# Crossbar transposes for a third of a batch, and VectorE steps merged over heads, tiles and spectra, in a fused attention and gated convolution

## The chip, the cores and the metric

The kernel runs on one core of a Trainium2 chip (trn2). The metric is device time in microseconds (us) of one execution, the median of several runs. The core has TensorE (matmuls and transposes, into PSUM banks), VectorE, ScalarE, GpSimd and SyncE, each with an instruction stream of its own that is worked off in order; they meet through semaphores. DMA engines move data between HBM and the on-chip memory (SBUF) and inside SBUF. Loads are issued here by GpSimd, stores and transposing copies by SyncE.

## What is computed

The reference is attention with a local window and a few global keys, followed by a long convolution with gates on both sides. There are 4 batches, 8 heads, 768 positions and 64 elements to a head, so a model width of 512.

```
scores = q @ k^T / sqrt(64) - slope[h] * dist       # kept: 0 <= i-j < 96, or j < 8
x      = concat over heads of softmax(scores) @ v    # (4, 768, 512)
x1, x2, x3 = split(x @ w_proj)                       # each (4, 768, 512)
c      = irfft(rfft(x2, axis=seq) * rfft(filter, axis=seq))
out    = (x1 * c * x3) @ w_out
```

## The kernel before

**Attention.** For each of four batches the 768 positions are worked in seven key tiles of 112 rows, in three groups `c`: tiles (0, 1), (2, 3), (4, 5, 6). q and k arrive as rows (`qn`, `kn`, one buffer each for all batches) and are needed with the head's elements on the partitions (`QT`, `KT`). `turned` (L672 and on) transposes them on TensorE (L679) into a PSUM bank and has VectorE or ScalarE copy them out (L309). `crossed` (L662 and on) has SyncE issue a DMA transpose instead (L669). `XB` (L207) names the (batch, group) pairs that go this way: the second and third group of the last batch. `scores` forms a key tile against its window of queries for two heads at a time, 64 rows each (L720), ScalarE takes the exponential (L748) into `E`, and VectorE multiplies by a mask that holds window, slopes and global keys (L760). In batch 0 the mask is added on TensorE instead (L707). `values` multiplies by v (L778, L783); VectorE takes the reciprocal of the sums (L808) and normalises (L802). Each v tile has the rows of the global keys below its own 112; a copy inside SBUF, issued by SyncE, puts them there once v's tile 0 has landed (`load_global`, L325 through `load`).

**Gates and convolution.** The normalised x is turned (L825, or by DMA, L835) into `xT`. `gate` multiplies xT by a 128-column tile of the first and third part of w_proj for one half of the positions (L870), has x1 and x3 copied out (L313, L879), and multiplies both on VectorE (L881). The convolution splits the sequence by symmetries (`butterfly`, L846 to L857), projects (L944), takes a small Fourier transform as matmuls (L634), copies six spectra out (`X`), multiplies by the filter's spectrum as complex numbers (`spectra`, L1081 to L1098), transforms back (L965, L968), mixes halves (L1036 to L1042), joins and multiplies by the gates (L1056 to L1061), and multiplies by w_out (L996). The filter's spectrum and the tables of sines are made in the kernel during batch 0.

**The order.** Nothing is scheduled at run time. The functions record operations with their reads and writes; `ORDER` (L40 to L88) is a list of them, one word each, such as `86P45`: operation 86, on TensorE, into PSUM banks 4 and 5. The word's letter also chooses VectorE or ScalarE where a copy can go to either. Each engine works its words in the order of the list, and GpSimd and SyncE issue their DMAs in that order. `i13b0` stands for thirteen dummy matmuls while the first loads are under way; a dummy exponential (`6A`, L371) brings ScalarE's table of exponentials back after the sines.

Of the kernel before, what the change touches and what calls it, by code (L numbers as in the profile page):

```python
# [16 lines left out]
P = 128  # L17
# [23 lines left out]
4V 0S 1A 2S 3A 21G 12V 13V 28V 10G 30A 29A 31A 15V 33V 11A i13b0 76P0 32A 34G 17G 19V 41G 18G 9V 40G 39G 42G 20V 66A  # L41
63A 24V 61A 72P1 46G 14V 35G 25V 70P2 26V 23A 22V 7G 64A 47G 73A 48G 45G 67A 60A 38G 77V 86P45 80V 74P3 52G 44G 90P01
43G 16V 75V 71A 78P2 79V 50G 49G 110P6 111V 51G 91P 81A 65A 62A 112P3 113A 88P 87P 89A 55G 261G 108P2 8V 219P6 220A
92P 93A 114P3 156P7 94P45 96P 109V 95P 27V 115V 122P23 262G 97A 69V 260G 221V 157V 214P0 82P45 259G 222V 123A 158P7
159V 84P 116P23 215A 216V 160P1 117A 83P 161V 120P67 53G 217V 154P1 5V 155V 118P23 258G 270G 85A 269G 121A 119A 268G
36S 267G 162P01 273G 98P67 275G 68V 99V 100V 37S 164P45 163A 165A 103P23 104V 105V 276G 166P67 167A 168P01 274G 124P23
125V 126V 129P45 130V 131V 56G 57G 169A 106P6 107A 101P7 102A 127P2 128V 175P01 176V 132P3 58G 133V 170P45 59G 139P3
145P2 263G 223A 54G 177V 178P0 171V 362P1 493G 492G 172V 173P4 224A 179V 227V 229P5 207V 226A 266G 277G 141A 174V
360P0 491G 272G 218A 134P3 208V 201V 271G 363A 230A 361A 364A 150P4 185P0 228V 186P1 358P7 489G 490G 147A 6A 278G 210V
200V 203V 188A 209V 231V 359V 202V 211V 225V 152A 181P2 136A 232A 140P1 369P67 142V 375P45 204V 183A 279G 143V 370A  # L50
390P3 135P2 388P1 499G 498G 212V 365A 501G 376A 500G 187V 137A 391V 389V 372P67 180P0 366P23 373A 392P45 191P1 138V
182A 374V 264S 434P0 436P6 367A 371V 393A 193A 395P23 189V 396A 510G 438P7 435V 205V 398P45 399A 196P0 437V 439V
449P67 450A 401P23 402A 198A 184V 507G 504G 206V 285P1 281P4 394V 213V 506G 286A 505G 283P5 446P23 440P01 397V 443P67
282A 447A 296P4 307P2 284A 298P3 297A 289P4 441A 299A 149P5 144P0 302P3 592P1 290A 400V 494G 151A 195P5 300P4 451V
509G 444A 265S 377V 368V 722G 146A 403V 234V 235V 236V 237V 383P67 448V 308A 190P0 502G 303A 238V 153V 301A 239V 148V
192A 384V 240V 197A 378P23 721G 385V 287P4 241P0 593A 590P5 242A 379V 409P67 723G 591A 194V 246P1 247A 380V 288A 442V
404P23 243P0 244A 248P5 726G 588P1 724S 410V 411V 199V 412P4 405V 249A 594V 719G 445V 406V 457P67 381P5 245V 595A 250V
407P0 589A 408A 382A 452P23 386P1 387A 458V 233V 459V 618P0 460P5 619A 453V 738G 413V 454V 251P67 252A 461V 496S 620P1
621V 508G 255P23 305V 253A 420P0 257A 455P1 292V 456V 256A 631P67 632A 605P45 294P3 422A 295A 414P1 416A 495S 664P0
254V 665A 304V 666P2 482V 668P3 667A 602P67 603A 735G 483V 669V 424P1 484V 306V 309P0 310A 478P2 425P3 528P0 280G 485V  # L60
291V 606A 679P45 486V 480A 426A 311V 427A 529A 676P67 419P2 677A 415P3 293V 417A 421A 511P0 607V 512A 312V 680A 487V
524P1 525A 313P0 462P2 418V 670P67 678V 428V 604V 681V 728G 599P45 464A 321P3 733G 323P1 314A 322A 600A 671A 515P2
315P3 516A 325P0 324V 317P1 318A 327P4 488V 326V 429P5 328A 497G 430P0 319P2 320A 431A 432A 601V 736G 513P1 514A 316V
628P23 633V 596P45 673P67 672V 597A 629A 730G 526P0 674A 329V 463P1 468P4 465A 330V 473P5 475A 625P23 626A 622P67 846S
734G 890S 821P1 848S 729G 527A 423V 331V 433V 732G 334V 727G 332V 472P5 623A 539P2 630V 477P3 519P0 845S 335V 333V
822V 847S 540A 467P1 520A 720G 474A 819P2 737G 338V 336V 470V 339V 469A 517P0 337V 479A 627V 537P5 518A 613P67 614V
820A 538A 349P1 350A 718G 598V 615V 889S 624V 675V 817P0 532P2 818A 340P5 503G 685P67 686V 824V 341A 533A 687A 608P01
609V 530P5 531A 823V 892S 610V 471V 891S 682P23 683V 476V 639P01 640V 684V 346P4 347A 634P67 616P5 617A 641V 828P23
829A 855P01 856A 635V 611P4 535V 343P5 893P23 688S 894A 636V 612V 481V 902P67 344A 852P01 355P4 903A 830V 853A 534V
637P2 541V 638V 642P3 643V 352P5 542V 649P3 689S 904V 356A 353A 834P67 835A 521V 825P01 826A 522V 854V 654P2 656A  # L70
655P5 739G 645P4 647A 644P6 690S 523V 657A 651A 466V 536V 659P2 661A 712V 711V 646A 648V 702P7 704A 714V 858P45 859A
896P23 713V 831P01 832A 697P6 857V 715V 345S 897A 543P7 707P4 709A 836V 557P5 555P0 556A 744P1 551P2 545P4 553P3 699A
716V 860V 348S 549P0 650P6 558A 550V 833V 554A 717V 827V 658V 725S 544A 552A 731G 547P5 342S 548A 546A 560V 559V 753P0
691P7 895V 849P45 652A 754A 850A 899P23 693A 900A 755P6 756A 660P0 745A 561V 837P45 838V 839A 740P7 851V 840P23 757P6
564V 701P1 841V 842V 662A 901V 843S 351S 703A 861P23 908P45 898V 905P01 741A 565V 862V 692P7 758A 909V 910A 863V 696P6
357S 906V 562V 864P23 907V 706P0 759P1 694A 563V 761P7 865V 866A 568V 742P4 743A 762A 766P5 768P2 569V 767A 844S 566V
911S 585P3 663V 354S 746P4 567V 760A 764V 867S 579P7 912S 748P1 769A 582P2 573P5 708A 763V 580A 868S 770V 749A 570P7
747A 583A 576P2 765V 705V 771V 750V 774P4 786P1 586A 782P3 571A 751V 913S 775A 778P7 870P0 710V 752V 577A 783A 787A
935V 934V 936V 772P2 780P4 773A 781A 937V 930P3 932A 776P2 777A 938V 872A 784P1 785A 885P4 880P3 958P0 779A 789V 945P7
939A 788V 940V 941P1 959A 946A 790V 791A 943P0 944A 653V 875P7 695V 942A 954P2 578S 955A 949P0 950A 793V 877A 956P1  # L80
957A 947P2 948A 572S 794V 792V 967P7 968A 587S 869P0 581S 969P1 970A 882A 795V 797V 924P2 796V 951V 971V 960P7 961A
952V 962P1 963A 925P3 871A 927A 879P7 881A 915P0 972V 953V 884P3 584S 965V 988P7 887A 964V 698A 574A 886A 966V 888V
973P6 974A 700V 992P4 993A 989A 873V 798V 805P1 994P6 995A 990P3 975P4 991A 997V 996V 977P5 978A 979P7 980A 874P6
802P3 808P7 883V 876A 799P6 998V 814P5 878V 976A 981V 982V 575S 999A 926A 914P2 806A 1001V 811P1 983V 984A 1002V 1000V
929P4 917A 815A 800A 801S 919P6 807S 986V 803A 809A 920P7 985V 987V 1005V 816S 810S 1003V 804S 1006V 812A 931A 1004V
1013P3 1018V 916A 813S 921A 933V 918V 922A 1007P2 1008A 1016V 1009S 923V 1014A 1015S 928V 1017V 1010P7 1019V 1020P2
1011V 1012S 1021V 1022S 1023P3 1024A 1026P7 1027A 1025S 1028S 1029P2 1030A 1031S
# [112 lines left out]
class Fused:  # L200
# [6 lines left out]
    XB = ((3, 1), (3, 2))  # L207
# [31 lines left out]
    def buffers(self):  # L239
# [30 lines left out]
        pp = t("pp", [P, 2, 4, DM])  # L270
        self.p1, self.p2 = ([pp[:, x, 2 * i:2 * i + 2] for i in range(2)] for x in range(2))
# [418 lines left out]
    def scores(self, hp, gi, near=False):  # L690
# [60 lines left out]
        if near:  # L751
            return
        mk = self.mask[:, 2 * hp:2 * hp + 2]
        if gi < 2:
            mk = mk[:, :, self.STEP * gi:self.STEP * (gi + 2)].rearrange("p h (t c) -> p h t c", t=2)[:, :, :, 0:n]
            w = 2 * W
        else:
            eo, mk = et[:, :, at:at + W + 16], mk[:, :, self.STEP:self.STEP + W + 16]
            w = 2 * (W + 16)
        g.op("V", dve(w, 2), lambda _: nc.vector.tensor_mul(eo, eo, mk),  # L760
             r=[("mask", 2 * hp), ("mask", 2 * hp + 1)], w=[("E", hp, gi)], name="masked")
# [98 lines left out]
    def gate(self, b, j, s):  # L860
        nc, g, h = self.nc, self.g, self.S // 2
        gt = self.gt[b % 2]
        xs = [("xT", i, c) for i in range(2) for c in ((0, 1) if s == 0 else (1, 2))]
        pts = []
        for o in (0, 2 * self.DM):
            bk = g.bank()

            def run(_, o=o, bk=bk):
                for c in range(4):
                    nc.tensor.matmul(bk.f32()[:, 0:h], self.w[:, c, o + P * j:o + P * j + P],  # L870
                                     self.xT[:, c, h * s:h * s + h], start=(c == 0), stop=(c == 3))
            g.op("P", pe(*[h] * 4), run, acq=[bk], r=xs + [("w", o // P + j)], name="gate")
            pts.append(bk)
        x1, key = self.x1[self.turn4 % 4], ("x1", self.turn4 % 4)
        self.turn4 += 1
        g.op("AV", self.evac(h), lambda e: self.times(e, x1, pts[0].f32()[:, 0:h], X1_SCALE),
             use=[pts[0]], w=[key], name="x1")
# [7 lines left out]
    def attention(self, b):  # L885
        self.b = b
        self.g.batch = (self.PERIOD * (b - 1 + self.SHIFT), self.PERIOD * self.LONG)
        for c in range(3):
# [18 lines left out]
            for i in range(4):  # L907
                self.scores(i, c, b == 0 and c < self.NEAR)
# [327 lines left out]
```

## Time and profile before

| | |
|---|---|
| median of 3 runs | 165.59 us (164.84 to 165.88) |
| the profiled execution | 165.6 us |
| its span, first to last instruction | 163.9 us |
| TensorE busy | 156.0 us, 95% |
| VectorE busy | 149.6 us, 91% |
| ScalarE busy | 149.7 us, 91% |
| GpSimd busy | 73.9 us, all before 82 us |
| granted TensorE clock | 1.00 throughout |

The profile names engines PE (TensorE matmuls), PEld (TensorE weight loads), DVE (VectorE), ACT (ScalarE), POOL (GpSimd) and SP (SyncE); a q behind the name (SPq) is the engine's queue that issues a DMA or waits. A line such as `PE bank L870` is work on the tile `bank`, recorded at line 870. The chain of waits follows back from the last instruction what each had to wait for; pieces in it have a start and a length in us. The list of waits tells which engine and line waited for which, the total in us, how often, and the longest. In a timeline each row has a start, a length, the engine, the line, the tile written and the tiles read, shapes, and how many instructions are merged. Busy time of TensorE is from modelled ends, so a busy TensorE may still be short of its full rate.

### The profile page before, as it was taken

The page shows a single profiled execution, that of the slowest core. Times are in us where ns is not written, and L with a number is a line of the kernel's source. Part 1 is how long each engine was busy: PE and PEld are TensorE (multiplying, and loading weights), DVE is VectorE, ACT ScalarE, POOL GpSimd, SP SyncE. Part 2 cuts the span into 40 slices and gives each one's busy share as a digit, 9 for nine tenths or more (in the row PEclk, how much of TensorE's full clock was granted, in tenths as well). Part 3 has the DMA queues.
Part 4 walks back from the last instruction along what each step waited for, and adds up shares of the span by engine and source line. Part 5 has one row for each costly group of instructions (what it writes and reads, how often), then busy time and mean ns, then how long its engine had stood idle before and what let it go on. Part 6 is the DMA issues. An engine that isn't in the chain of part 4 may idle for free.

```text
span 163.9 us, 4281 instructions
## 1 busy us (share of the span) xinstructions
PE 156.0 (95%) x1619; PEld 95.3 (58%) x1619; DVE 149.6 (91%) x339; ACT 149.7 (91%) x325; POOL 73.9 (45%) x101
## 2 busy tenths in 40 slices
PE   6798999999999999899999999999999999999990
PEld 2455678665456875455566755665754654574550
DVE  3788869999999999999999999999999999999970
ACT  4688899999999999999999999999999798999931
POOL 7999999985599999978700000000000000000000
PEclk9999999999999999999999999999999999999999
DMA  4999999999999999999995545000444270010586
GB/s 109 196 147 125 166 172 166 158 173 206 178 173 158 153 150 146 140 172 155 156 139 102 76 93 184 14 0 4 130 128 107 78 270 0 4 64 0 206 326 238
DMA packets 91684, 21.97 MB, mean 134 GB/s; under 512 B 84288, under 2 KB 88720, under 8 KB 91664
## 3 DMA queue, kind: packets, MB, share of 16 engines
q0 software_dynamic: 74960, 11.82, 98.7%
q1 hardware_dynamic: 14624, 9.37, 21.0%
q10 hardware_dynamic: 2080, 0.52, 1.8%
q8 instruction: 12, 0.20, 0.4%
q14 instruction: 8, 0.07, 0.1%
HBM read 24.64 MB, written 6.29 MB: 189 GB/s over the span
## 4 chain that ended last, share of the span: by engine, by line
PE 55%; DVE 25%; POOL 6%; ACT 5%; DMA 4%; issue 2%; POOLq 0%; ACTq 0%; DVEq 0%
PE bank L870 16%; PE bank L996 12%; PE bank L944 8%; DVE E L760 5%; PE bank L634 4%; DMA qn<-in_q_dram 4%; DVE xn L802 3%; PE bank L720 3%; PE bank L778 3%; PE bank L965 3%; POOL kn L325 3%; PE bank L783 2%; PE bank L707 2%; ACT E L748 1%; DVE xT L309 1%
## 5 line engine op out<-in xcount | busy, mean ns | idle before, releaser
L870 PE MATMUL bank<-xT,w 128*128 128x384 f16 x256 | 48.5, 326 | 0.6 <-DVE KT L309 0.6
L748 ACT ACTIVATE E<-bank 128x832 f16<-128x832 f32 (+2 forms) x64 | 44.6, 785 | 1.2 <-PE bank L720 1.2
L870 PEld LDWEIGHTS <-w 128*128 128x128 f16 x256 | 23.6, 98 | 17.1 <-issue 1.9
L325 POOL DMA_DIRECT2D vn<-in_v_dram x28 | 23.4, 852 | 4.0 <-DMA wo<-in_moe_w_out_dram 1.7
L325 POOL DMA_DIRECT2D kn<-in_k_dram x27 | 22.7, 866 | 0.7 <-issue 0.3
L996 PE MATMUL bank<-wo,y 128*128 128x512 f16 (+1 forms) x100 | 22.9, 370 | 0.0
L760 DVE TENSOR_TENSOR E<-E,mask 128x832 f16<-128x832 f16 (+1 forms) x36 | 21.4, 617 | 0.4 <-ACT E L748 0.4
L325 POOL DMA_DIRECT2D qn<-in_q_dram x21 | 19.0, 920 | 1.4 <-PE bank L944 1.4
L879 ACT CAST g<-bank 128x384 f16<-128x384 f32 x30 | 15.8, 542 | 0.3 <-PE bank L870 0.3
L313 ACT ACTIVATE x<-bank 128x384 f16<-128x384 f32 x31 | 16.1, 548 | 0.0
L313 ACT ACTIVATE ot<-bank 128x512 f32<-128x512 f32 (+1 forms) x23 | 12.9, 608 | 3.1 <-PE bank L996 1.9
L802 DVE TENSOR_TENSOR xn<-bank,rc 128x512 f16<-128x512 f32 (+1 forms) x20 | 15.2, 763 | 0.2
L778 PE MATMUL bank<-vn,E 128*128 128x65 f16 x224 | 15.3, 193 | 0.0
L313 ACT ACTIVATE ab<-bank 128x512 f16<-128x512 f32 x24 | 15.1, 688 | 0.1
L996 PEld LDWEIGHTS <-y 128*128 128x128 f16 x100 | 9.4, 98 | 9.9 <-issue 0.3
L778 PEld LDWEIGHTS <-E 128*128 128x128 f16 x224 | 14.0, 97 | 1.9
L783 PE MATMUL bank<-vn,E 128*128 128x65 f16 x192 | 15.0, 193 | 0.0
L720 PE MATMUL bank<-QT,KT 64*128 64x208 f16 (+1 forms) x224 | 14.9, 245 | 0.0
L309 ACT CAST X<-bank 128x512 f16<-128x512 f32 x24 | 14.0, 659 | 0.1
L783 PEld LDWEIGHTS <-E 128*128 128x128 f16 x192 | 13.2, 97 | 0.8 <-issue 0.2
L309 ACT CAST eo<-bank 128x384 f16<-128x384 f32 x28 | 12.4, 566 | 0.8 <-PE bank L968 0.8
L720 PEld LDWEIGHTS <-KT 64*128 64x128 f16 x224 | 8.4, 94 | 6.4 <-issue 3.9
(158 smaller groups left out, 337.4 us busy)
## 6 DMA issues: line engine op xcount, KB each, us to landing
out_dram<-ot SPq DMA_DIRECT2D x23, 256.0 KB, 2.5
qn<-in_q_dram POOLq DMA_DIRECT2D x21, 128.0 KB, 5.7
vn<-in_v_dram POOLq DMA_DIRECT2D x24, 112.0 KB, 5.7
kn<-in_k_dram POOLq DMA_DIRECT2D x23, 112.0 KB, 5.6
w<-in_moe_w_proj_dram POOLq DMA_DIRECT2D x4, 256.0 KB, 6.4
ot<-in_q_dram ACTq DMA_DIRECT2D x2, 256.0 KB
w<-in_moe_w_proj_dram POOLq DMA_DIRECT2D x1, 512.0 KB, 7.8
wo<-in_moe_w_out_dram POOLq DMA_DIRECT2D x1, 512.0 KB, 8.1
```

What stands on the lines that cost most here:

```text
L309: {"A": nc.scalar.copy, "V": nc.vector.tensor_copy, "G": nc.gpsimd.tensor_copy}[e](out, in_)
L313: self.nc.scalar.mul(out, in_, c)
L325: return self.g.op(eng, 0.57 + 0.00035 * nbytes[0] if eng == "G" else 0.5, lambda _: e.dma_start(dst, src), w=w, r=r, nbytes=nbytes, name= ...
L720: nc.tensor.matmul(bs[hh].f32()[:, off:off + w], self.KT[hs, hp, P * m:P * m + P], self.QT[hs, hp, KL * m:KL * m + w], start=(off == 0 and ...
L748: nc.scalar.activation(dst, src(), Act.Exp, scale=self.scale)
L760: g.op("V", dve(w, 2), lambda _: nc.vector.tensor_mul(eo, eo, mk), r=[("mask", 2 * hp), ("mask", 2 * hp + 1)], w=[("E", hp, gi)], name="ma ...
L778: nc.tensor.matmul(o[:, n, hh], ef[:, at:at + P], vt[:, t, 2 * hp + hh, 0:D + 1], start=first, stop=(t == 0), skip_group_check=True)
L783: nc.tensor.matmul(o[:, n, hh], ef[:, at:at + P], vt[:, t - 1, 2 * hp + hh, 0:D + 1], start=False, stop=True, skip_group_check=True)
L802: nc.vector.tensor_mul(to, o[:, :, :, 0:D].rearrange("p i (t h) d -> p i t h d", h=2), rc.rearrange("p i (t h) o -> p i t h o", h=2).to_br ...
L870: nc.tensor.matmul(bk.f32()[:, 0:h], self.w[:, c, o + P * j:o + P * j + P], self.xT[:, c, h * s:h * s + h], start=(c == 0), stop=(c == 3))
L879: first = g.op("AV", {"A": act(h), "V": 0.0005}, lambda e: nc.scalar.copy(x3, pts[1].f32()[:, 0:h]) if e == "A" else None, use=[pts[1]], w ...
L996: nc.tensor.matmul(bk.f32()[:, 0:cw], y[:, c, P * t:P * t + P], self.wo[:, c, cs], start=(c == 0), stop=(c == 3))
```

## The change

Five things change.

1. `XB` takes in the first group of the last batch, so its three q tiles and two k tiles are transposed by DMA.
2. The mask of one group is multiplied into `E` for four heads in one VectorE instruction, instead of two heads. It moves from `scores` to a function of its own, `masked`.
3. `gate` handles two column tiles at once: four matmul blocks, four copies to SBUF, and one VectorE product of twice the length. A product straight from PSUM, possible before, is not left.
4. The complex products of a batch run over the four spectra 0 to 3 in one instruction each, instead of over pairs: two products and one sum of 2048 elements. They follow all four spectra. The spectra 4 and 5 keep their two products.
5. `ORDER` is another one from beginning to end, with other choices of engine and bank.

```diff
-    XB = ((3, 1), (3, 2))
+    XB = ((3, 0), (3, 1), (3, 2))
...
+    def masked(self, j, gi):
+        t0, n, W = self.GRP[gi][0], self.N, self.GW[gi]
+        et, mk = (x[:, 4 * j:4 * j + 4] for x in (self.EE.rearrange("p i h c -> p (i h) c"), self.mask))
...
+        self.g.op("V", dve(w, 2), lambda _: self.nc.vector.tensor_mul(et, et, mk),
+                  r=[("mask", 4 * j + i) for i in range(4)], w=[("E", 2 * j + i, gi) for i in range(2)], name="masked")
...
-    def gate(self, b, j, s):
+    def gate(self, b, jp, s):
...
+        for j in range(2 * jp, 2 * jp + 2):
...
+            g.op("AV", self.evac(h), lambda e, x3=x3, bk=pts[1]: self.copy(e, x3, bk.f32()[:, 0:h]),
+                 use=[pts[1]], w=[("g", b % 2, j, s)], name="x3")
+        x3 = gt[:, js, h * s:h * s + h]
+        g.op("V", dve(2 * h, 2), lambda _: nc.vector.tensor_mul(x3, x3, self.x1p[:, k:k + 2]),
+             r=[("x1", k + i) for i in range(2)], w=[("g", b % 2, j, s) for j in range(2 * jp, 2 * jp + 2)], name="g")
...
         self.spectra(b, (2, 3))
+        self.products(False)
         self.spectra(b, (4, 5))
+        self.products(True)
...
+    def products(self, real):
+        nc, g, X, DM = self.nc, self.g, self.X, self.DM
+        ss = (4, 5) if real else (0, 1, 2, 3)
+        ks, xs = [("X", s) for s in ss], X[:, ss[0]:ss[-1] + 1]
...
+        g.op("V", dve(2048, 2), lambda _: nc.vector.tensor_mul(
+            p1, xs, self.h1[:, 0:4:2][:, :, None].to_broadcast([P, 2, 2, DM])), r=rs, w=[("p1", 0), ("p1", 1)], name="prod")
+        g.op("V", dve(2048, 2), lambda _: nc.vector.tensor_mul(p2, xs, hs), r=rs, w=[("p2", 0), ("p2", 1)], name="prod")
+        g.op("V", dve(2048, 2), lambda _: nc.vector.tensor_add(xs, p1, p2[:, :, ::-1]),
+             r=[(k, i) for k in ("p1", "p2") for i in range(2)], w=ks, name="sums")
```

The start of the two orders (the first words):

```diff
-4V 0S 1A 2S 3A 21G 12V 13V 28V 10G 30A 29A 31A 15V 33V 11A i13b0 76P0 32A 34G 17G 19V 41G 18G 9V 40G 39G 42G 20V 66A
+4V 0S 1A 2S 3A 28V 15V 10G 11V 17G 18G 19V 5V 30V 20V 23A 64A 13V 34G 42G 21G 24A 40G 39G 41G 48G 47G 29A 32A 45G 46G
+25V 26V 33V 35G 36S 38G 54G 22A 16V 67A i13b0 76P0 62A 63A 31V 60A 7G 44G 77A 43G 12V 81A 50G 72P1 94P23 73V 70P4 74P0
```

Here 34G is the load of k tile 1, 41G, 42G, 46G, 47G and 48G those of k tiles 2 to 6, 39G, 40G and 45G those of q tiles 3 to 5, 35G and 38G those of v tiles 0 and 1, and 36S the first copy of the global rows of v. 21G makes the far mask, 10G the identity, 18G the distances.

## The prediction

> **What bounds the kernel now.** I read the busy sums of the page, then the table of stretches, then the chain of waits, then who waits for whom. The first two lines are from the page and from the stretches (columns: span, busy us of TensorE, weight loads, VectorE, ScalarE, GpSimd, granted clock, DMA share, GB/s); the stretch shown is typical of all from 75 to 155 us.
>
> ```profile
> PE 156.0 (95%) x1619; PEld 95.3 (58%) x1619; DVE 149.6 (91%) x339; ACT 149.7 (91%) x325; POOL 73.9 (45%) x101
> 105.00:115.00 10.00, 10.00 (x103) 6.26 (x101) 9.92 (x21) 10.00 (x26) 0.00 (x0) 1.00 0.01 2
> ```
>
> Three engines are full at once, so shares don't decide; the chain does. Its pieces in order of time:
>
> ```profile
> 74.47 0.48 DVE eo L309
> 74.99 0.33 PE bank L965 x3
> ...
> 82.05 0.50 PE bank L679 x8
> ...
> 85.15 0.22 PE bank L679 x4
> ...
> 87.44 0.45 PE bank L679 x8
> ...
> 148.03 3.45 PE bank L996 x16
> ```
>
> From 75 us to the last matmul at 160.0 every piece is TensorE. It runs at its rate: 16 matmuls of 512 columns in 3.45 us are 0.216 us each, as in the other runs of this line. From 37.5 to 75 the chain is VectorE, yet TensorE loses little there. Who TensorE waited for, longest first, after the dummy matmuls at the start:
>
> ```profile
> PE bank L870 <- DVE KT L309: 0.6, 1, 0.6
> PE bank L679 <- DVE KT L309: 0.6, 1, 0.6
> PE bank L965 <- DVE eo L309: 0.2, 1, 0.2
> PE bank L679 <- DMA qn<-in_q_dram: 0.2, 1, 0.2
> ```
>
> With the waits of its weight loads for VectorE (0.2 to 0.3 each, seven of them) no more than 2.7 us are lost after 24 us. So the time is TensorE's work, the point at which it can start on the attention, and a tail; lighter VectorE and ScalarE can give back at most those 2.7 us.
>
> **Part 1, the crossbar.** For the last batch twelve transposes of 128x128 (q) and eight of 112x112 (k) leave TensorE: the three L679 pieces above, 0.50+0.22+0.45 = **-1.17 us**, on the path. Three evacuations go too. Added are five DMA transposes on SP, 1.21 us (KT) and 1.26 us (QT) each on the queue; their median landing is 2.4 and 3.4 us. In the changed order SP holds eleven q and k transposes in a row, behind two copies of the global v rows and ahead of batch 2's xT transposes and batch 0's first store. Nine are ahead of the first scores of batch 3, and five of these (QT4, KT1, KT0, QT3, QT1) come after one that must wait for batch 2's last scores, or are that one. So the scores' data is there 5 x 1.26 + 3.4 = 9.7 us after those scores. TensorE has in between five gates (5 x 0.65), six value blocks (3.16), eight spectral matmuls (1.73), two output tiles (1.73) and two transpose blocks (0.40): 10.3 us. Cover 0.6 us: cost **0**; with the slowest landing of the line (4.2 us) 0.2 us late. The copies of the global keys wait for KT0, third of the five (3 x 1.26 + 2.4 = 6.2 us); on VectorE the normalisations of batch 2 queue behind it, beside TensorE work 9 us after the same point. The loads: 17 followed wo's from 66.1 to 81.1 us, 0.88 each; now 23 follow, so wo's is near 60.8 and the last one needed (k tile 1, thirteenth after it) is issued near 72 and lands 5.7 us later, at 78, before the transposes that need it at 83. Hidden.
>
> **Part 2, the merged VectorE steps.** The chain has the step from one instruction to the next:
>
> ```profile
> 64.95 0.87 DVE xab L848
> ...
> 66.09 0.60 DVE xcf L851
> ```
>
> 1536 elements 0.87, 1024 elements 0.60: 0.27 per 512, so 0.07 are fixed. Masks go from 36 to 18, gate products from 32 to 16, complex products and sums from 24 to 12: 46 x 0.07 = 3.2 us of VectorE. The evacuations move too (VectorE gets one normalisation that ScalarE did in 16 pieces of 0.20 us; ScalarE loses four 512-column q copies of 0.47 us): about 3 us less on VectorE and 4 us less on ScalarE in sum. All of it lies beside TensorE. What it can return is the 2.7 us of waits; what it can cost is longer waits: a mask waits for the exponentials of four heads, a gate product for four evacuations, the first product for all four spectra. Each merge makes the first consumer up to one old step later (0.5 to 0.6 us). I take **-0.6 us**, near a fifth of the waits, between -2.7 and +1.7 (rival A).
>
> **Part 3, the order on TensorE.** Scores use 64 rows, all else 128. The timeline has the start of each piece:
>
> ```profile
> 93.33 0.36 PE L825 MATMUL bank<-ident,xn 112*128 112x112 f16 x4
> 93.62 0.53 PE L720 MATMUL bank<-QT,KT 64*128 64x208 f16 x8
> 94.08 0.37 PE L825 MATMUL bank<-ident,xn 112*128 112x112 f16 x4
> ```
>
> Four transposes of 112 columns start 0.05 apart, so the scores could start at 93.53, and start 0.1 late. Eight matmuls of 208 columns, two at a time, are 4 x 0.088 = 0.35 us; the next work comes 0.46 after their start. So one group costs 0.21 us over its columns; a group of 10 (0.51) and of 14 (0.68, 0.56 of it columns) say the same. The order had 30 groups with scores, the changed one 34: **+0.84 us**, between 0 and that. The Trainium skill, "TensorEngine Tiling (Array Packing)", Key Properties, says that changing the tiling mode drains TensorE: by that rule the price is one for each group, as counted; were it a price of each matmul, the 0.84 would fall away.
>
> **Part 4, the start.** On GpSimd's queue the first v tile now comes behind all of batch 0's k and q loads. The old start:
>
> ```profile
> 7.30 1.65 POOL L325 DMA_DIRECT2D kn<-in_k_dram  x2
> 8.93 0.82 POOL L325 DMA_DIRECT2D vn<-in_v_dram  x1
> ...
> 10.47 1.59 POOL L325 DMA_DIRECT2D kn<-in_k_dram  x2
> 12.05 0.91 POOL L325 DMA_DIRECT2D qn<-in_q_dram  x1
> ```
>
> The rows of GpSimd's timeline in the new order: 0.80 to begin, identity 0.51, row number 0.10, distances 1.13, two k 1.7, far mask 1.19, two q 1.78, three k 2.46, q 0.88, k 0.82: v at 11.4 instead of 8.9. It landed 3.8 us after its issue, now at 15.2. Behind it is SP's copy of the global rows into v, which landed 5.6 us after its own:
>
> ```profile
> vn<-vn SPq DMA_DIRECT2D x1, 48.0 KB, 5.6
> ```
>
> So the first values can't start before 20.8. They started at 19.69, when TensorE had nothing older left; TensorE now reaches them earlier, near 18.6, since one block of the angle matmuls (14.14 to 14.67, 0.53 us) is queued behind instead of ahead. Work that is behind stays to be done: +1.1 and +0.5, **+1.6 us**. Bounds: no wait at all (0), and 5.9 us for the copy and 0.6 more for v (+2.5). The q and k tiles land up to 2 us earlier, which only lengthens that wait.
>
> **Small ones.** The last gate of all ends 2.6 us before the output matmuls that need its product; ScalarE 0.8, product 0.47, two y*g of 0.47 fill 2.2 of it, much as now: 0. The dummy exponential that brought its table back (1.28 us) goes to the end; the next exponential loads the table instead: 0, or +1.3 if a load comes up at the end.
>
> **Sum.** The profiled execution took 165.6 us, span 163.9 and 1.7 around it, the median of the runs shown (165.59). 165.6 - 1.17 + 0.84 + 1.6 - 0.6 = **166.3 us**. What a measurement of this kernel can tell is about 1%, 1.7 us: no change.
>
> **The rivals.**
> *A, one long product chain (slower, 168.6, chance 0.24).* Place: the inverse transforms, eight in a row behind one sum. In batch 0 VectorE has between the last xT copy of batch 1 and that sum two butterflies of 0.87, two products and the sum of 1.13 (0.60 + 2 x 0.27), six steps of 0.60, and 2.5 of small ones: 11.7 us with the copy. TensorE has 12.4 us of other work queued (six projections of 0.86, five gates, the rest spectra, scores, transposes). It decides from 0.7 us that VectorE is behind there (1.0 in the later batches: 5.0 of filler on TensorE for 4.0 of evacuation, products and sum in the last). With VectorE 1.5 us behind in each, TensorE waits 0.8 and three times 0.5: 2.3 on top of the forecast. For: VectorE was the chain from 37.5 to 75. Against: it has 3 us less to do.
> *B, the waits melt (164.2, chance 0.17).* The copy of the global rows meets less traffic and lands 1 us sooner, and half of the 2.7 us go: 166.3 - 1.0 - 1.1. For: ScalarE and VectorE are both lighter. Against: they were lighter than TensorE before, too.
> *C, SP is late (168, chance 0.06).* The cover of 0.6 us is gone, and xT of batch 2 behind it; 4.2 us landings and one more place in the queue give 0.2 + 1.3. Against: eight such transposes kept 1.2 us steps at 82 to 93 us.
> *D, the long steps hold the loads (168, chance 0.03).* GpSimd's load issues of k and v took 0.82 to 0.83 us before 20 us and 0.87 to 0.89 at 50 to 70 us, beside a full VectorE. Steps of twice the length that make this 0.12 on each of 60 loads delay the last by 7 us, 2 more than the 5 by which it is ahead. The Trainium skill, "SBUF — State Buffer", two separate sides, says that VectorE's two-port modes lock GpSimd out of writing descriptors; a step of 1.13 us would then hold one load 1.1 us. The rows show 0.06.
>
> **The numbers.** The forecast (within 165.0 to 167.6) has 0.50. Below 163.9 (faster by over 1%) lie the better half of B and a little of the forecast: 0.10. Above 167.3: A, C, D less their mild ends, and the forecast's upper end: 0.31. Within: 0.59. The range leaves out 0.1 on each side: 163.9 to 168.8.
>
> **What would show it.** Right: no L679 at 80 to 88 us and 1599 matmuls; the first value matmul near 20.8, with the copy of v into itself as what TensorE waited for; 34 groups of scores at 0.21; VectorE's busy sum 3 to 4 us lower and ScalarE's 4; TensorE's waits after 24 us near 2; three table loads. Wrong: a first value matmul before 19.7; TensorE waiting for VectorE's X before the inverse (A); for QT or KT with SP's transposes late (C). The forecast fails most easily through Part 4, one wait worked out from one landing, and through waits of the new order that no row of the old one shows.

## The result and the profile after

The changed kernel takes **175.43 us** (median of 4 runs, 173.24 to 180.07), the kernel before 165.49 us beside it (164.84 to 165.88): a ratio of **1.057** (95% interval 1.051 to 1.064). The forecast was 166.3 us, no change. The ratio leaves out the longest execution, 180.07 us, which is the one that was profiled; its span is 178.4 us. The four executions had mean granted clocks of 0.986, 0.978, 0.967 and 0.961, in the order 173.24, 175.34, 175.52 and 180.07 us, where the kernel before had 1.00.

The page of the changed kernel, busy sums, then TensorE's row of busy tenths and the row of the granted clock over 40 slices of 4.46 us:

```profile
PE 161.5 (91%) x1599; PEld 95.1 (53%) x1599; DVE 148.7 (83%) x293; ACT 147.7 (83%) x309; POOL 73.9 (41%) x101
...
PE   7999199999999999999988059999999999999991
...
PEclk9999858999999999999999957999999999999999
```

The same two rows before, over 40 slices of 4.10 us:

```profile
PE   6798999999999999899999999999999999999990
PEclk9999999999999999999999999999999999999999
```

TensorE has 20 matmuls fewer, as the change says, and is busy 5.5 us longer. The rows show why: there are two holes in its work that were not there before, in the 5th slice and in slices 23 and 24 (with a dent ahead of the second, in 21 and 22), and behind each the clock falls, so that the same matmuls take longer. The list of waits of TensorE, longest first, names the holes:

```profile
PE bank L719 <- DMA QT<-qn: 6.0, 1, 6.0
PE bank L777 <- DMA vn<-vn: 3.8, 1, 3.8
PE bank L777 <- DVE E L759: 1.4, 1, 1.4
```

The first scores of batch 3 wait for a crossbar transpose (QT), and the first values for the copy of the global rows into v. From the chain of waits of the same execution (start, length in us, what):

```profile
17.29 4.83 DMA vn<-vn
...
86.17 8.66 DMA vn<-in_v_dram
95.35 8.87 DMA QT<-qn
...
169.28 5.20 PE bank L1000 x28
```

Before, the chain from 75 us on was TensorE and nothing else. Now it goes through a v load and the transpose of QT 1, which landed 8.87 us after SP issued it. The stretches behind that wait (columns as in the prediction; the granted clock is third from the end):

```profile
95.00:100.00 5.00, 3.35 (x82) 2.81 (x78) 1.62 (x5) 2.11 (x5) 0.00 (x0) 1.00 1.76 154
100.00:105.00 5.00, 0.64 (x5) 0.29 (x6) 3.15 (x6) 0.63 (x3) 0.00 (x0) 0.78 1.63 140
105.00:110.00 5.00, 5.00 (x20) 1.43 (x20) 2.96 (x3) 2.87 (x5) 0.00 (x0) 0.53 0.21 69
```

From 105 to 110 us TensorE is full again, at 0.53 of its clock, and finishes 20 matmuls. Cut into stretches of 1 us, the clock is 0.50 from 20.9 to 27.7 us and from 102.8 to 109.7 us, 6.8 us each time. TensorE is still idle in the first 1.4 and 1.5 us of these, and loses half of the rest: 2.7 us each, on top of the wait. So the profiled time comes out as first values 2.6 us later than before (22.26 against 19.69), 2.7 for the clock, first scores of batch 3 held 6.0, and 2.7 for the clock: 14.0. The spans differ by 14.5.

### The profile page after: what moved, and what is told of

It reads as the page before. It is cut to its first block, busy times and chain, and to the rows that moved or that the text cites. A ratio compares the mean times of both kernels' runs of the same rounds, so it can differ in the third digit from the quotient of the medians.

```text
span 178.4 us, 4185 instructions
## 1 busy us (share of the span) xinstructions
PE 161.5 (91%) x1599; PEld 95.1 (53%) x1599; DVE 148.7 (83%) x293; ACT 147.7 (83%) x309; POOL 73.9 (41%) x101
## 4 chain that ended last, share of the span: by engine, by line
PE 66%; DMA 17%; POOL 6%; DVE 5%; ACT 1%; issue 1%; SPq 0%; DVEq 0%
PE bank L872 17%; PE bank L1000 12%; PE bank L946 8%; PE bank L719 5%; DMA QT<-qn 5%; DMA vn<-in_v_dram 5%; DMA wo<-in_moe_w_out_dram 5%; PE bank L633 4%; PE bank L304 3%; PE bank L678 3%; POOL vn L324 3%; PE bank L777 3%; DMA vn<-vn 3%; PE bank L706 2%; PE bank L969 2%; PE bank L782 2%
## 5 line engine op out<-in xcount | busy, mean ns | idle before, releaser
L747 ACT ACTIVATE E<-bank 128x832 f16<-128x832 f32 (+2 forms) x64 | 45.4, 819 | 7.8 <-PE bank L719 7.7
L1000 PE MATMUL bank<-wo,y 128*128 128x512 f16 (+1 forms) x100 | 24.7, 390 | 0.0
L719 PE MATMUL bank<-QT,KT 64*128 64x208 f16 (+1 forms) x224 | 16.1, 254 | 6.0 <-DMA QT<-qn 6.0
L777 PE MATMUL bank<-vn,E 128*128 128x65 f16 x224 | 15.9, 197 | 5.2 <-DMA vn<-vn 3.8
L759 DVE TENSOR_TENSOR E<-E,mask 128x1664 f16<-128x1664 f16 (+1 forms) x18 | 19.3, 1087 | 0.0
L777 PEld LDWEIGHTS <-E 128*128 128x128 f16 x224 | 14.5, 100 | 7.6 <-issue 4.2
L312 ACT ACTIVATE ot<-bank 128x512 f32<-128x512 f32 (+1 forms) x24 | 14.1, 614 | 5.4 <-PE bank L1000 4.7
L308 ACT CAST g<-bank 128x384 f16<-128x384 f32 x31 | 17.4, 567 | 0.4 <-PE bank L872 0.2
L312 ACT ACTIVATE x<-bank 128x384 f16<-128x384 f32 x31 | 16.3, 567 | 0.7 <-PE bank L872 0.7
L719 PEld LDWEIGHTS <-KT 64*128 64x128 f16 x224 | 8.6, 97 | 15.1 <-issue 13.0
L801 DVE TENSOR_TENSOR xn<-bank,rc 128x512 f16<-128x512 f32 (+1 forms) x21 | 16.3, 786 | 0.3
L308 ACT CAST X<-bank 128x512 f16<-128x512 f32 x24 | 14.9, 661 | 0.8 <-PE bank L633 0.7
L782 PE MATMUL bank<-vn,E 128*128 128x65 f16 x192 | 15.6, 195 | 0.0
L782 PEld LDWEIGHTS <-E 128*128 128x128 f16 x192 | 13.5, 99 | 0.6
```

The costliest lines, as they stand in the source:

```text
L308: {"A": nc.scalar.copy, "V": nc.vector.tensor_copy, "G": nc.gpsimd.tensor_copy}[e](out, in_)
L312: self.nc.scalar.mul(out, in_, c)
L719: nc.tensor.matmul(bs[hh].f32()[:, off:off + w], self.KT[hs, hp, P * m:P * m + P], self.QT[hs, hp, KL * m:KL * m + w], start=(off == 0 and ...
L747: nc.scalar.activation(dst, src(), Act.Exp, scale=self.scale)
L759: self.g.op("V", dve(w, 2), lambda _: self.nc.vector.tensor_mul(et, et, mk), r=[("mask", 4 * j + i) for i in range(4)], w=[("E", 2 * j + i ...
L777: nc.tensor.matmul(o[:, n, hh], ef[:, at:at + P], vt[:, t, 2 * hp + hh, 0:D + 1], start=first, stop=(t == 0), skip_group_check=True)
```

## The experiments

All numbers beside a run are medians; the kernel before took 165.1 to 165.5 us beside each.

| kernel | us | range | ratio (95% interval) |
|---|---|---|---|
| changed, once more | 176.8 | 174.2 to 177.6 | 1.062 (1.049 to 1.075) |
| first v load early | 173.8 | 173.7 to 175.1 | 1.054 (1.047 to 1.061) |
| dummies in both waits | 178.2 | 176.8 to 178.8 | 1.078 (1.069 to 1.086) |
| part 1 undone | 169.2 | 168.3 to 173.7 | 1.020 (1.010 to 1.030) |
| loads reordered | 171.9 | 168.4 to 172.7 | no interval |
| QT 1 first | 176.8 | 171.4 to 177.6 | no interval |
| loads reordered, steps split | 173.1 | 169.9 to 175.3 | 1.035 (1.026 to 1.043) |
| dummies before the scores only | 173.9 | 172.0 to 175.9 | 1.047 (1.040 to 1.054) |
| part 1 alone in the kernel before | 170.2 | 169.5 to 170.4 | 1.028 (1.023 to 1.032) |
| ten v loads left out | 167.6 | 166.3 to 170.0 | no interval |
| both queues repaired | 166.2 | 164.4 to 167.3 | 1.002 (0.998 to 1.005) |
| repaired, steps split | 167.8 | 166.8 to 169.4 | 1.013 (1.010 to 1.017) |
| repaired, part 1 undone | 168.7 | 167.9 to 169.0 | 1.020 (1.017 to 1.022) |

### Two waits, or one cause?

The changed kernel unchanged, and three edits of it.

> The changed kernel once more, for a second profile of it. Theory 1 (two idle spells of TensorE, each with a cause of its own and each followed by some 6.6 us at half the granted clock, 3.3 us lost): 173 to 180 us, with TensorE idle near 18.5 to 22.3 us for the copy of the global rows of v and near 98 to 104 us for QT, and a granted clock of 0.5 behind both. The second spell is near the length that still counts, so its loss may be there in one execution and not in the next, which would give the spread of the times. Theory 3 (the low clock has nothing to do with idle time): the low clock lies elsewhere in this profile.

The second profile (span 172.5 us) has only the second of the two long waits, and GpSimd's:

```profile
PE bank L719 <- DMA QT<-qn: 5.9, 1, 5.9
POOL kn L324 <- PE bank L678: 5.0, 1, 5.0
...
PE bank L777 <- DMA vn<-vn: 0.4, 1, 0.4
```

The copy of the global rows landed at 19.4 us here and at 22.1 in the first profile. So the wait at the start comes and goes, while that for QT stays. TensorE stood before the scores at 93.09 us; the kernel before began them at 93.62, so up to there the changed kernel was, if anything, ahead; from its first scores of batch 3 on, each of the two has 554 matmuls left. It began them at 98.95 and ended 8.5 us later than before. Of these, 5.3 are the late scores, and 2.2 are the half clock (from 98.95 to 103.4). About 1 us is left: from these scores to its end TensorE is busy 69.7 us against 66.6, of which the half clock explains 2.2. Where the rest comes from is open.

```profile
95.00:100.00 5.00, 1.05 (x6) 0.45 (x7) 3.35 (x7) 1.24 (x3) 0.00 (x0) 0.66 1.61 136
100.00:105.00 5.00, 5.00 (x28) 1.67 (x26) 2.96 (x3) 3.29 (x6) 0.00 (x0) 0.66 0.29 81
```

The first v load early, one word moved:

```diff
-40G 39G 41G 48G 47G ... 45G 46G ... 35G 36S 38G
+40G 39G 41G 35G 48G 47G ... 45G 46G ... 36S 38G
```

> The changed kernel with one word of the order moved: the load of the first v tile is issued behind batch 0's third k load, as it was before the change (five loads earlier, at about 8.8 us instead of 11.4). Both theories: it lands near 13, its copy near 18.5, first value matmul near 19.7 instead of 22.3, no idle spell of 3.8 us and no half clock at 22 to 28 us: 2.5 + 3.3 = 5.8 us less. Theory 1: the wait for QT near 98 us has a cause of its own and stays at 4 to 6 us, now near 93 us, with the half clock behind it: about 170 us. Theory 2 (one cause: the late start makes everything behind it late, the loads of batch 3 among it): that wait goes too, 165 to 166 us.

The load was issued at 8.1 us and landed at 11.9, the copy at 16.1, the first value matmul came at 18.65 without a wait. The wait for QT was not touched:

```profile
PE bank L719 <- DMA QT<-qn: 6.4, 1, 6.4
PE bank L777 <- DMA vn<-vn: 1.6, 1, 1.6
```

Theory 2 falls: the second wait is not the first one handed on. (The 1.6 us is the same copy for batch 1.) At 173.8 us the kernel gains 1.6 and 3.0 us on the two medians of the changed one, not 5.8. The 5.8 were worked out from the longest execution, and its first wait is not typical: the eight profiles taken here of kernels with the changed kernel's start and no dummies in the way have it as 3.8, 2.7, 2.5, 1.5, 1.0, 0.4 and 0.4 us, and once not at all. The spread of the times is 1.5 us here.

Part 1 undone, 20 transposes and three evacuations back in the order near where SP's words were:

```diff
-XB = ((3, 0), (3, 1), (3, 2))
+XB = ((3, 1), (3, 2))
```

> The changed kernel with part 1 undone: the first third of batch 3's q and k goes through TensorE again (20 transposes, three evacuations), the five transposes on SP are gone, all else of the order stands. Theory 1: the first idle spell and its half clock stay, the wait for QT (6 us) and the half clock behind it (3.3) go, 1.2 us of transposes come back: 8 us less, 167 to 168 us by the median of the changed kernel, 172 by its profiled execution. Theory 2 (all from the late start): the loads are as late as before and TensorE waits for them in its own transposes instead: 174 to 176 us.

As theory 1 had it, the wait for QT is gone, and with it 6 to 8 us: 169.2. Eight transposes are left. Those issued from 79.9 to 85.7 us still land 6.6 to 7.4 us later where the profile has their landing, beside loads that land until 96.4 us, but TensorE never waits for them. The last two, issued behind 102 us with the loads done, land 2.6 us after their issue.

### The clock

Dummy matmuls ahead of the first values and of batch 3's first scores:

```diff
+i15b5   (ahead of 98P23)
+i24b6   (ahead of 791P67)
```

> The changed kernel with 15 dummy matmuls of 512 columns (15 x 0.216 = 3.2 us) ahead of the first value matmuls and 24 (5.2 us) ahead of batch 3's first scores, so that TensorE works through most of both idle spells without doing anything useful. Theory 1: the granted clock stays at 1.00, the two waits end when they did, and up to 2 x 3.3 us come back: 169 to 170 us. Theory 3 (the low clock is not caused by idle time): clock as low as before at the same places, 175 us or, with the dummies in the way, up to 177.

This went wrong twice. The copy had landed at 20.8 us, but the 15 dummies went on until the first values came at 21.62: they filled the wait and made it longer. And the 24 stood behind a PSUM bank that a normalisation on VectorE still held: TensorE was idle from 95.5 to 97.6 us before them, and the clock fell at 98.0, after 2.07 us of idleness. Eight of the dummies then ran at half speed, and they went on to 104.2 us: QT had landed at 100.3, and the scores began at 104.55 only. So the run doesn't show a gain, but it shows that 2 us were enough for the low clock. The Trainium skill, "TensorE: Matmul & The Clock Gate", "Why this matters for your kernels", asks for no idle gap over about 3 us; here a gap of 2.07 us was already too long.

The second dummies alone, on a bank that is free in time:

```diff
+i24b3   (ahead of 791P67)
```

> The changed kernel with 24 dummy matmuls of 512 columns (5.2 us) ahead of batch 3's first scores alone, on a bank that is free in time, so that TensorE is busy through most of its wait for QT. If the low clock comes from idle time: no half clock behind the wait, QT lands when it did, 3.4 us come back: 171 to 173 us, and less often the slow times above 175. If not: 174 to 177.

Now the wait for QT is filled with dummies (96.4 to 101.6 us), the scores begin at 101.73, and the clock behind them is 1.00. In the same execution an idle spell of 1.52 us ahead of the first values was followed by half clock:

```profile
95.00:100.00 5.00, 5.00 (x59) 2.99 (x57) 2.83 (x7) 1.78 (x4) 0.00 (x0) 1.00 1.76 129
100.00:105.00 5.00, 5.00 (x35) 1.97 (x35) 2.26 (x4) 2.82 (x5) 0.00 (x0) 1.00 0.99 113
...
18.00:23.00 5.00, 3.48 (x39) 1.79 (x34) 3.19 (x7) 2.17 (x5) 4.85 (x7) 0.69 1.91 164
```

So the low clock comes from idle time, and work without a use keeps it away. The four executions have mean clocks of 0.980 to 1.000, the eight of the changed kernel 0.961 to 0.986. The time is 173.9 us against 175.4 and 176.8 in the two series of the changed kernel; the intervals of the ratios overlap, so a gain of 1.6 to 2.9 us is not certain. The effect on the clock is clear.

### What made QT late

SP's queue in the second profile of the changed kernel (start, time on the queue):

```profile
76.98 1.37 SPq L668 DMA_TRANSPOSE QT<-qn  x1
78.93 3.41 SPq L668 DMA_TRANSPOSE KT<-kn  x2
82.44 2.85 SPq L668 DMA_TRANSPOSE QT<-qn  x2
85.38 3.56 SPq L668 DMA_TRANSPOSE KT<-kn  x2
89.04 2.63 SPq L668 DMA_TRANSPOSE QT<-qn  x2
91.83 1.20 SPq L668 DMA_TRANSPOSE KT<-kn  x1
93.31 1.21 SPq L668 DMA_TRANSPOSE QT<-qn  x1
```

Ten places in 16.3 us (76.98 to 93.31), 1.6 on the mean where the prediction had 1.26; and the list of DMA issues of the same kernel (count, median us to landing) has

```profile
KT<-kn SPq DMA_TRANSPOSE x7, 7.9
QT<-qn SPq DMA_TRANSPOSE x6, 8.0
```

where the kernel before had

```profile
KT<-kn SPq DMA_TRANSPOSE x5, 2.4
QT<-qn SPq DMA_TRANSPOSE x3, 3.4
```

(The list counts two transposes of k more than the row of eleven; they come later.) Two theories: the loads that run beside them (theory 4), or the row of eleven itself (theory 5). GpSimd's loads are late since the k 3 load of batch 3 writes over rows that batch 2's transposes still read; that is the 5.0 us wait above, 9.0 in the first profile. The last load was issued at 86.8 us instead of 80.3, and landed at 99.8 instead of 85.6. The loads in an order without that wait, words of batch 3 on GpSimd's queue:

```diff
-700G 690G 698G 276G 480G 697G 699G 693G 688G 493G 704G 701G 709G 706G 691G 689G 692G
+690G 698G 276G 480G 697G 693G 688G 691G 689G 692G 700G 699G 493G 704G 701G 709G 706G
```

(700, 699, 704 and 706 are k 3, 2, 4 and 6, 276 is wo.)

> The changed kernel with GpSimd's loads of batch 3 in another order and nothing else: the k tiles whose places are still read by batch 2's transposes (k 3, 2, 4, 5, 6) come behind the loads that need not wait (q 2, q 4, output weights, v 1 of batch 2, q 3, v 0, q 0, k 0, q 1, k 1). GpSimd then does not stand 5 us before the k 3 load. Theory 4 (SP's transposes land 8 us after their issue because the loads that were held up run at the same time on the same DMA engines, and SP itself starts late because its copy of batch 3's v rows waits for the v 0 load): the last load is issued near 82 us instead of 87, SP's first transpose starts near 72 instead of 77, the landings fall to 3 to 5 us, QT 1 is there before TensorE asks for it near 93 us, the idle spell of 5.9 us and the half clock behind it go: 165 to 167 us. Theory 5 (eleven crossbar transposes in a row are slow by themselves, whatever else the DMA engines do): landings stay at 7 to 8 us, the wait shrinks by 2 to 3 us at most: 170 to 173 us.

```profile
PE bank L719 <- DMA QT<-qn: 3.5, 1, 3.5
...
POOL kn L324 <- PE bank L678: 2.3, 1, 2.3
```

171.9 us, a wait of 3.5 us and median landings of 5.2 (KT) and 7.0 us (QT) look like theory 5. But the loads still landed until 94.3 us, and SP's second transpose, KT 3, stood until 81.1 us for batch 2's scores, which read the rows it writes. So it doesn't tell the two apart.

QT 1 moved up on SP's queue:

```diff
-784S 812S 811S 786S 810S 788S 787S 809S 785S 852S 849S
+784S 812S 811S 786S 785S 810S 788S 787S 809S 852S 849S
```

> The changed kernel with one word of SP's order moved: the transpose of QT 1, on which batch 3's first scores wait, goes ahead of those of QT 4, KT 1, KT 0 and QT 3, four places up. It is then issued near 84 us instead of 90. If each transpose lands a fixed 8 us after its own issue, the last of the five that the first scores need is now KT 0, one place behind the old fourth, 1.4 us earlier than QT 1 was: the wait of TensorE is 4.5 instead of 5.9 us, 1.4 us less in all. If they all land together when the loads let them, the wait stays: 174 to 177 us. Under neither does the half clock go, which would need the idle spell near 3 us or less.

No gain on the median (176.8, against 175.4 and 176.8): KT 0 is the last one now, and VectorE's copy of the global keys waits for it. The first row of VectorE's timeline in this kernel says so, with the idle time before it in brackets:

```profile
100.81 0.18 DVE L308 COPY KT<-KT 128x64 f16<-128x64 f16 x1 [5.46 <-DMA KT<-kn]
100.90 0.95 DVE L801 TENSOR_TENSOR xn<-bank,rc 128x768 f16<-128x768 f32 x1
```

Behind it is the normalisation that frees the scores' bank. TensorE waited 5.3 us. Moving one transpose up only makes another the last.

Part 1 alone, in the kernel before, with two q loads moved up (817, 820, 821 are QT 0, KT 0 and KT 1, 818 and 819 QT 1 and QT 2):

```diff
-XB = ((3, 1), (3, 2))
+XB = ((3, 0), (3, 1), (3, 2))
...
+817S 820S 821S 818S 819S   (on SP, ahead of the eight)
-817P0 818A 819P2 820A 821P1 822V
```

> The kernel before, with part 1 alone: five transposes on SP in place of 20 on TensorE and three evacuations, on SP ahead of the eight that were there, and the loads of q 0 and q 2 of batch 3 moved up on GpSimd's queue, so that they are there in time. Nothing is merged and the rest of the order stands. My prediction had part 1 at 1.2 us less: 164 us. If thirteen transposes in a row beside the loads land 7 us after their issue, the eight old ones come 6.5 + 3 us later than they did and batch 3's second scores wait 1 to 3 us, with 1.7 us of half clock behind it: 166 to 169 us.

170.2 us, 4.6 more than before, worse than either guess. Waits of TensorE that the kernel before doesn't have:

```profile
PE bank L720 <- DMA KT<-kn: 2.2, 1, 2.2
...
PE bank L720 <- DMA QT<-qn: 1.0, 1, 1.0
```

Half clock followed (98.3 to 101.7 us). This run also hints at the answer: its loads ended at 87.9 us; transposes issued at 79.0 and 80.5 us landed 6.9 and 7.6 us later, those issued from 90 us on 2.3 to 3.4 us later.

To settle it, ten v loads taken away with the row left as it is. The value matmuls of two batches then read older rows, so this kernel leaves out part of the result; it serves for its times alone:

```diff
+OUT = ((2, 2), (2, 3), (2, 4), (2, 5), (3, 1), (3, 2), (3, 3), (3, 4), (3, 5), (3, 6))
...
+        if what[0] == "vn" and (b, t) in self.OUT:      # recorded, but issues nothing
```

> The changed kernel without ten of the v loads that run beside SP's transposes (tiles 2 to 5 of batch 2 and 1 to 6 of batch 3; the value matmuls of these two batches work on the v rows of the two batches before, so this part of the result is left out, all instructions on the other engines stay). The order of SP and of TensorE is unchanged, and GpSimd still stands before the k 3 load. Theory 4 (the transposes land late because the loads share the DMA engines): the landings of the eleven transposes fall from 7 to 8 us to 3 to 4, SP is not held back while it issues them, QT 1 lands near 92 to 93 us, the wait of 5.9 us falls under 1.5 and the half clock behind it goes: 166 to 169 us. Theory 5 (a row of eleven is slow by itself): landings stay at 7 to 8 us, the wait stays over 4 us: 173 to 177.

```profile
KT<-kn SPq DMA_TRANSPOSE x7, 3.5
QT<-qn SPq DMA_TRANSPOSE x6, 3.1
```

Theory 4 holds and theory 5 falls: the medians of the same row fall to 3.1 and 3.5 us, nearly all of the eleven take 1.2 to 1.3 us on the queue as in the kernel before, and TensorE's list of waits has no QT on it. The last load is now issued at 77.6 and landed at 84.2 us, so that the later half of the row has no load beside it. The first transpose, issued at 77.8 us while loads were still landing, took 6.6 us. 167.6 us (166.3 where the clock stayed at 1.00, 168.9 and 170.0 where it was 0.98). The slow transposes are those that run beside GpSimd's loads. The loads land later in turn: the last v load took 13.0 us in the second profile (86.8 to 99.8), against 5.4 in the kernel before and 7.4 there with part 1 alone.

### Both queues put right

The reordered loads, the early v load, and on SP the five transposes that the first scores need ahead of the others (SP's words):

```diff
-695S 478S 784S 812S 811S 786S 810S 788S 787S 809S 785S 852S 849S 660S 661S 347S 694S
+478S 784S 787S 788S 785S 786S 812S 811S 810S 809S 852S 849S 660S 661S 347S 695S 694S
```

> The changed kernel with all its parts, its matmuls in the same order, and three queues put right: GpSimd's loads of batch 3 as in the reordered kernel, the first v tile's load five places earlier, and on SP the five transposes that batch 3's first scores need (QT 0, KT 0, KT 1, QT 1, QT 2) ahead of the other six, with the copy of batch 3's own v rows behind them. The five are issued from about 70 to 81 us; with landings of 7 to 8 us, as measured, they are there by 89, TensorE asks at 93. Theory 4, in the form that is left (the loss is the wait for QT, made by the order of the queues and by slow landings beside late loads, and the half clock behind it): no idle spell over 2 us, clock 1.00, 163.5 to 166 us. If the changed order of TensorE or the merged steps cost several us by themselves, it stays at 168 or more.

166.2 us, 1.002 of the kernel before (0.998 to 1.005). TensorE's waits are back to those of before:

```profile
PE bank L646 <- DMA ot<-in_k_dram: 1.5, 1, 1.5
PE bank L304 <- DVE idle L368: 1.3, 1, 1.3
PE bank L719 <- DMA QT<-qn: 0.6, 1, 0.6
PE bank L678 <- DVE KT L308: 0.5, 1, 0.5
```

Transposes still land 7.8 to 8.1 us after their issue, on the median, but the five are issued from 71.5 to 79.2 us and the last is there at 87.8, before the first scores ask for it at 91.4. (The 0.6 us is for one of the other six, which landed 9.6 us after its issue.) So the whole loss of the change, as far as these times can tell, lay in the order in which GpSimd and SP issue their DMAs. No arithmetic and no matmul's place had to change to get it back. It is also the best version found: as fast as the kernel before, not faster.

### What parts 1 and 2 are worth without the waits

Each merged step issued as two, for instance the mask:

```diff
-lambda _: self.nc.vector.tensor_mul(et, et, mk),
+lambda _: [self.nc.vector.tensor_mul(et[:, i:i + 2], et[:, i:i + 2], mk[:, i:i + 2]) for i in (0, 2)],
```

> The repaired kernel with each merged VectorE step issued as two of half the size, one right behind the other (46 more instructions, 46 x 0.07 = 3.2 us more of VectorE). What part 2 of my prediction is worth when no wait for QT covers it: by the prediction the time rises by 0.6 us (bounds: 1.7 more to 2.7 less); if VectorE's lighter load lies wholly beside TensorE it stays within 0.3 us of the repaired kernel.

167.8 us against 166.2; the intervals of the two ratios don't overlap. The split steps cost 1.6 us. Three groups of steps in the repaired kernel (masks, gate products, one of the complex products; busy us, mean ns of one):

```profile
L759 DVE TENSOR_TENSOR E<-E,mask 128x1664 f16<-128x1664 f16 x12 | 12.0, 1018 | 0.0
L883 DVE TENSOR_TENSOR g<-g,x 128x768 f16<-128x768 f16 x16 | 8.7, 547 | 0.0
L1090 DVE TENSOR_TENSOR pp<-X,h 128x2048 f16<-128x2048 f16 x4 | 4.9, 1216 | 0.0
```

and split:

```profile
L759 DVE TENSOR_TENSOR E<-E,mask 128x832 f16<-128x832 f16 x24 | 12.8, 583 | 0.0
L884 DVE TENSOR_TENSOR g<-g,x 128x384 f16<-128x384 f16 x32 | 9.8, 349 | 0.0
L1091 DVE TENSOR_TENSOR pp<-X,h 128x1024 f16<-128x1024 f16 x8 | 5.1, 682 | 0.0
```

VectorE's busy sum rises from 148.5 to 151.2, 2.7 us for 46 instructions. The profile doesn't tell where TensorE loses the 1.6 us: it is of the longest execution, 169.4 us, and its longest wait, 2.7 us, is for a load of k near 18 us, which the split doesn't touch. The same edit to the kernel with reordered loads:

> The kernel with the reordered loads, and in it each merged VectorE step issued as the two of half the size that it replaced, one right behind the other (masks 18 to 36, gate products 16 to 32, complex products and sums 12 to 24): the waits of the merged form stay, only the 46 fixed parts come back. VectorE's busy sum rises by 46 x 0.07 = 3.2 us. My prediction had the merges at 0.6 us less in the end: slower than the reordered kernel by 0 to 1 us. A merge that holds up what is behind it would show as a faster kernel here, since the first half is done 0.5 us earlier.

173.1 against 171.9, with overlapping ranges: the same sign, but no evidence by itself. Part 1 undone in the repaired kernel, the 20 transposes in the gaps near their old places:

> The repaired kernel with part 1 undone: 20 transposes and three evacuations back on TensorE, VectorE and ScalarE, the five transposes on SP gone, the rest as it stands. What part 1 of my prediction is worth when the transposes are covered: 1.2 us more than the repaired kernel. If TensorE then waits for the evacuations, or if the five transposes still cost something in the repaired kernel (0.6 us of waiting for QT in its profile), the difference is 0.6 us or less.

168.7 us, 2.4 more by the medians. TensorE's busy sum is 1.2 us longer (156.6 against 155.4), its added work. The rest is waiting for what feeds the blocks, 0.8 us at 45 to 60 us and 1.6 more at 87 to 95 us in the profiles, where the transposes were put in by hand; so of the 2.4 only the added work can safely be put down to part 1. Both parts bring something in this order, and yet the order with both is no faster than the old one with neither. The new order itself must then cost about what they save; no run has the new order without both.

## Why the prediction was wrong

**What bounds: right.** TensorE is the path, and up to the scores of batch 3 the second profile of the changed kernel was even with the kernel before.

**Part 1: this step failed, in its cover.** The 1.17 us of transposes do leave TensorE (TensorE's busy sum is 1.2 longer in the run that puts them back). But "five places and a landing", 5 x 1.26 + 3.4 = 9.7 us, measured 15.1 (QT 4 issued at 83.76, QT 1 landed at 98.81 in the second profile): 1.6 more for the four places from QT 4 to QT 1, since SP was held back while it issued them, and 3.8 more for the landing, 8.4 instead of 3.4 and one place. The time that TensorE had in between was 9.3, near the 10.3 estimated. 15.1 less 9.3 is 5.8, the wait of 5.9. Behind the wrong size is a wrong statement: that the loads were hidden. I counted the loads behind wo and asked when each would be issued, but not whether GpSimd would stand in between. With the k 3 load it stood 5.0 us; wo went out at 64.5 us instead of the 60.8 forecast, k tile 1 at 76.8 instead of 72. (I also counted 17 loads behind wo in the kernel before; there are 15, and a wait of 1.7 us for wo between them. Counted rightly, wo would have been forecast still earlier.) And I asked whether the loads were in time for the transposes, not whether the transposes could share the engines with them. The landings of 2.4 to 4.2 us that I took came from rows at 82 to 92 us, where the loads were just ending; the profile before showed the last one landing at 85.6.

**The half clock: missing altogether.** The prediction priced a wait at its length. Each of these waits cost 2.2 to 2.7 us more. The forecast's own wait before the first values, 2.2 us by its numbers (18.6 to 20.8), could have been long enough. The kernel before shows no low clock after its first 5 us, its waits from there on being 1.1 us once, at 7 us, and 0.6 at most after that.

**Part 2: right in sign, too small.** -0.6 was taken; the split shows -1.6 in the repaired order, within the bounds. VectorE's sum didn't fall by 3 to 4 us as said but by 0.9 (1.1 in the repaired kernel): the merges give 2.7, other choices of engine take most of it back. ScalarE fell by 2.0 and not 4.

**Part 3: not contradicted.** There are 34 groups of scores, and a group of eight takes 0.46 us from its start to the next block's as before (80.56 to 81.02 in the first profile). TensorE's busy sum in the repaired kernel, at full clock, is 155.4 us against 156.0; -1.17 + 0.84 is -0.33. No run prices the change between 64 and 128 rows by itself.

**Part 4: right in mechanism, in its size only on the mean.** In the profiles of the changed kernel the v load, issued at 11.4 as forecast, landed at 15.7 and 17.2, its copy at 19.4 and 22.1, and the first values came at 19.5 and 22.3 (forecast 20.8). What was not seen is that this varies from one execution to the next and that the longer cases pull the clock down.

**The rivals.** A did not happen: before the inverse TensorE waits 0.3 us once, against 0.2. B did not. C named the right queue and the right wait (QT late, SP's transposes late), with a landing of 4.2 us instead of 8.4 and no clock: 168 instead of 175. The 0.6 us of cover that it doubted was the right place to doubt. D did not: the issues of the k and v loads take 0.85 and 0.83 us on the mean beside the longer VectorE steps, against 0.87 and 0.85. The lock of which the Trainium skill speaks ("SBUF — State Buffer", two separate sides) shows no price here. That page states it for VectorE's two-port modes, and no row here says whether the merged products run in one. Three table loads, as said.

## What to carry to other kernels

The time to landing of the transposes here depended on what else the DMA engines did then (2.4 to 9.6 us): take such a number from rows with the same traffic beside it, and move the loads in the plan before using the number. On every queue that an edit reorders, look for the first entry that must wait for another engine; all behind it move by that wait, and their landings shift into other traffic. And price a wait of TensorE of 2 us or more at its length plus up to half of 3.4 or 6.8 us (here 2.2 to 2.7 us); from about 1.1 us on the half clock can follow.

## What the runs showed of the hardware

**The half clock comes in steps of 3.4 us.** In all profiles the low clock inside the kernel lasts 3.4 or 6.8 us (102.8 to 109.7 in the first profile, 96.6 to 103.4 in the second, 98.0 to 101.4 with both dummies). It begins and ends on a grid of 3.41 us that is fixed within an execution: in the first profile it begins at 20.92 and at 102.84 us, which is 24 steps of 3.413. The Trainium skill, "TensorE: Matmul & The Clock Gate", Part 1, gives a free-running window of 3413 ns; the traces agree. By its phase the same kernel can lose a window more or less. That fits much of the spread from 173 to 180 us: a mean clock of 0.986 means 4.8 us at half clock, one of 0.961 means 13.9. A grid window with 2.1 us or more of idle TensorE was followed by half clock wherever work came after it; below 1.1 us it never was; between, both happened (1.1 and 1.5 us ahead of the first values: half clock; 1.6 us at 47 to 50 us in the kernel with the early v load: not). What decides there is open. The page of the kernel before prints a clock of 1.00 throughout, yet its first eight dummies take 3.60 us, 0.45 each, where 512 columns later take 0.216: for most of the first 5 us TensorE ran at half rate there too, which the printed clock doesn't show.

**Crossbar transposes are slow beside GpSimd's loads.** 3.1 to 3.5 us to landing without ten of these loads, 7.9 to 8.0 with them, though the transposes are issued by another engine on a queue of their own. How the two get in each other's way, and how much of the loads' own delay comes from the transposes, the runs don't show.
